# A list scheduler's cost numbers set to the durations of the profile, in a kernel of attention, experts and a dense network

## The chip, the cores and the metric

One core of one Trainium2 chip runs the kernel. The metric is the device time of one execution in microseconds (us); lower is better. Engines are named as in the profile: PE is TensorE (PEld its weight loads), ACT ScalarE, DVE VectorE, POOL GpSimd, SP SyncE, and a `q` behind a name is the engine's instruction queue.

## The reference

Three parts follow each other. `x` has 8 batches of 8 heads with 512 rows of 64 columns, `state` 32 rows for each head; the 8 x 544 rows that come out of the attention are the 4352 tokens of the rest.

```python
# attention, both ways, scale = 1 / sqrt(64)
a = softmax(scale * x @ state.T);   xread = a @ state
a2 = softmax(scale * state @ x.T);  sread = a2 @ x
x = concat([xread, sread], rows)                   # 4352 tokens of 512
# one expert of 8 for each token
logits = normalise(x) @ normalise(expert_emb).T / tau
e = argmax(logits);  gate = softmax(logits)[e]
x = gate * (relu(x @ w1[e]) @ w2[e])               # 512 -> 1024 -> 512
# dense network, for every token
h = x @ w_in                                       # 512 -> 2048
out = (h * clip(h + 3, 0, 6) / 6) @ w_out          # 2048 -> 512
```

All is float32, but `w_in` and `w_out`, which are float64.

## The kernel before

Big products are made of float32r parts: each operand is split in a high and a low part, and a product is three matmuls, high by high, low by high and high by low. So every operand costs a copy or cast that gives the high part (`wh`, `hx`, `yh`, `gh`, the first of `xt`) and a subtraction that gives the low part (`wl`, `yw`, `gl`, the second of `xt`).

**Stages.** The attention goes batch by batch, up to some 140 us. The routing then sorts the tokens by expert into slots of 128. The leading slots (`QUAD`, four slots, and `FIFTH`) are those of the expert with most tokens. The main units (`RUN`, one or two slots of one expert) follow: the products of `w1` (`L1w` line 1409, `L1` line 1450 for single slots), the relu and its split (`hx`, lines 1428 and 1432), the products of `w2` (`L2`, line 1512), the result times its gate (`yt`) and its store to `ysd` in sorted order (line 1540 on SP for the leading slots, line 1543 on POOL for the others). Beside them goes the dense network on blocks of 256 sorted tokens: load `yl` (line 1579), transpose (1585), split (`yh` 1594, `yw` 1597), `F1` (`u_ps`, line 1618), the activation (`r` 1622, `u_ps` 1625, `gh` 1629, `gl` 1632), `F2` (`o`, line 1653), and the result's scatter. What is left of the dense network when the units are done follows alone.

**Weights.** An expert's weights come as loads of `raw` (`load_w`, lines 1225 to 1252; the DMA on SP, line 1231 for `w1`, line 1234 for `w2`), through a ring of two buffers. Each load gives two pieces: `wh` (line 1245, by ACT or DVE) and `wl` (line 1248, by DVE or POOL), in a ring of three. The dense weights are converted once in 32 pieces (`convert`, lines 301 to 316): exponent and mantissa of the float64 are taken apart (lines 271 and 272 on DVE, 276 and 277 on ACT), multiplied (281 and 282 on DVE), summed (286, DVE or POOL) and split (293 ACT, 296 DVE or POOL). Eight of them come beside the attention, the others later.

**Tokens of a slot** (`X`, lines 1257 to 1384) are gathered by POOL (`xg` line 1270, in quarters `xq` line 1276) and turned into columns: by PE from a copy `xp` (line 1297) in the leading slots, by DVE's transposes of 32 x 32 (line 1314) in the others, whose cast `xt` (line 1325) goes to ACT or DVE and whose low part (line 1329) to DVE.

**What sets the order.** The kernel's instructions are written by a list scheduler (`Sched`, lines 39 to 151) that runs when the program is built. Every operation is given to it as `op(function, cost, priority, dependencies, buffers taken, buffers given, ...)`. The cost names the engine and a time in us; where it names two engines, the scheduler chooses. Each step takes the operation with the least key, where `b` is the time at which its operands, its buffers and its engine are ready by the scheduler's own clocks:

```python
key = (b + (c if len(o.cost) > 1 else 0.0) + self.wp * o.prio, o.prio)
```

It then sets `clk[e] = b + cost`, and the operation's end that much and `sem` later. For a DMA on SP's or ACT's queue the cost has a second meaning (line 142):

```python
self.hw = b + 0.45 * (1 + o.cost[e] // 0.12)
```

This is the time until which no other such DMA is issued: 0.45 us at a cost of 0.06, 1.8 us at 0.45. The priorities come from a nominal order (`at_`, `OFF`, `w_at`, `f1_at`) with numbers of its own.

## Time and profile before

| | |
|---|---|
| Runs | 1454.6 us median of 3 (1453.09 to 1455.71) |
| Span of the profiled execution | 1453.4 us, 1.2 us under the median |
| PE busy | 1354.7 us, 93% of the span |
| DVE busy | 917.8 us, 63% |
| ACT busy | 645.3 us, 44% |
| POOL busy | 543.1 us, 37% |

Only the span of the profiled execution is known, so it stands beside the median. The shares are means over stages that differ: the window table cuts the span into stages, with the busy time and, in brackets, the number of instructions of each engine. A line of a wait table names who waited, for whom, how long in total, how many times and the longest. A timeline's row has start, length, engine, line and operation, with idle time before it and its releaser in square brackets. A group of instructions by form has its busy time and the mean length of one in ns; a line's own table has least, median and greatest.

### The profile page before, as it was taken

How to read it: one execution, taken by the hardware profiler on the slowest of the kernel's cores; microseconds unless marked ns; L12 is line 12 of the kernel's file. 1: busy time of each engine (PE TensorE's matmuls, PEld its weight loads, DVE VectorE, ACT ScalarE, POOL GpSimd, SP SyncE). 2: the span in 40 equal slices, each digit the busy share in tenths (PEclk: the TensorE clock that was granted, in tenths of full speed). 3: DMA queues.
4: the chain of work that ended last, by engine and by line, in shares of the span. 5: the costliest groups of instructions: out<-in, count | busy, mean ns of one | idle time of the engine just before them, and what ended most of it. 6: DMA issues, size and time to landing. Idle time of an engine off the chain costs nothing. (4 is left out here: it accounts for less than half of the span.)

```text
span 1453.4 us, 25243 instructions
## 1 busy us (share of the span) xinstructions
PE 1354.7 (93%) x8976; PEld 1199.0 (82%) x8976; DVE 917.8 (63%) x2008; ACT 645.3 (44%) x1347; POOL 543.1 (37%) x558
## 2 busy tenths in 40 slices
PE   7896697877799999999999999999999999999997
PEld 6675686766688898989989898999998999899996
DVE  6988888899976555645454544665666675433332
ACT  4785435555643343434444343555544444333332
POOL 5554448566555232524142322244344322200000
PEclk8996689899899999999999999999999999999999
DMA  6643435555564333423243333555455544201000
GB/s 162 175 160 116 148 96 161 156 188 159 157 182 149 94 115 89 136 82 124 90 125 98 108 104 100 154 150 177 152 148 153 174 139 140 74 23 30 15 16 15
DMA packets 151765, 175.64 MB, mean 121 GB/s; under 512 B 43784, under 2 KB 116488, under 8 KB 150608
## 3 DMA queue, kind: packets, MB, share of 16 engines
q1 hardware_dynamic: 128544, 121.19, 28.2%
q0 software_dynamic: 12336, 35.99, 8.2%
q10 hardware_dynamic: 10752, 16.78, 3.6%
q8 instruction: 73, 1.20, 0.4%
q14 instruction: 60, 0.49, 0.1%
HBM read 146.09 MB, written 27.82 MB: 120 GB/s over the span
## 5 line engine op out<-in xcount | busy, mean ns | idle before, releaser
L1618 PE MATMUL u_ps<-yh,wih 128*128 128x256 f32 x1088 | 306.9, 282 | 6.0 <-DVE gl L1632 4.3
L1618 PE MATMUL u_ps<-yh,wil 128*128 128x256 f32 x1088 | 306.8, 282 | 3.1 <-DVE wil L296 3.1
L1618 PE MATMUL u_ps<-yw,wih 128*128 128x256 f32 x1088 | 307.0, 282 | 0.0
L1248 POOL TENSOR_TENSOR wl<-raw,wh 128x512 fp32r<-128x512 f32 x129 | 176.6, 1373 | 274.4 <-ACT wh L1245 127.3
L1625 DVE SCALAR_TENSOR_TENSOR u_ps<-r,u_ps 128x256 f32<-128x256 f32 x272 | 116.2, 427 | 255.0 <-ACT r L1622 240.5
L1622 ACT ACTIVATE r<-u_ps,three 128x256 f32<-128x256 f32 x272 | 129.1, 475 | 305.4 <-PE u_ps L1618 277.2
L1618 PEld LDWEIGHTS u_ps<-yh,wih 128*128 128x128 f32 x1088 | 207.3, 191 | 17.2 <-DVE gl L1632 4.3
L1653 PE MATMUL o<-woh,gh 128*128 128x512 f32 x544 | 217.0, 399 | 2.0 <-DVE yo L1667 1.2
L1653 PE MATMUL o<-wol,gh 128*128 128x512 f32 x544 | 216.4, 398 | 0.0
L1653 PE MATMUL o<-woh,gl 128*128 128x512 f32 x544 | 214.9, 395 | 0.0
L1618 PEld LDWEIGHTS u_ps<-yw,wih 128*128 128x128 f32 x1088 | 206.6, 190 | 8.5
L1618 PEld LDWEIGHTS u_ps<-yh,wil 128*128 128x128 f32 x1088 | 207.5, 191 | 3.3 <-DVE wil L296 3.3
L1512 PE MATMUL y_ps<-wh,hx 128*128 128x512 f32 x512 | 186.3, 403 | 1.3 <-DVE wh L1245 1.3
L1629 ACT CAST gh<-u_ps 128x256 fp32r<-128x256 f32 x272 | 101.2, 372 | 187.9 <-PE o L1653 140.4
L1248 DVE TENSOR_TENSOR wl<-raw,wh 128x512 fp32r<-128x512 f32 x223 | 160.5, 727 | 33.4 <-ACT wh L1245 29.6
L1632 DVE TENSOR_TENSOR gl<-u_ps,gh 128x256 fp32r<-128x256 f32 x272 | 114.4, 421 | 98.0 <-ACT gh L1629 94.3
L1276 POOL DMA_INDIRECT xq<-xd,qidx x128 | 136.1, 1063 | 54.0 <-issue 31.9
L1245 ACT CAST wh<-raw 128x512 fp32r<-128x512 f32 x197 | 120.9, 619 | 73.3 <-PE y_ps L1512 39.8
L1409 PE MATMUL h_ps<-xt,wh 128*128 128x256 f32 x704 | 140.9, 288 | 3.8 <-ACT wh L1245 3.8
L1672 POOL DMA_INDIRECT out_dram<-yo,ix x34 | 35.9, 1057 | 273.3 <-ACT gh L1629 160.0
L1653 PEld LDWEIGHTS o<-woh,gl 128*128 128x128 f32 x544 | 102.6, 189 | 25.2
L1409 PEld LDWEIGHTS h_ps<-xt,wh 128*128 128x128 f32 x704 | 117.6, 197 | 5.7 <-ACT wh L1245 4.2
(312 smaller groups left out, 2474.2 us busy)
## 6 DMA issues: line engine op xcount, KB each, us to landing
raw<-in_moe_w_dram SPq DMA_DIRECT2D x176, 512.0 KB
yl<-ysd SPq DMA_DIRECT2D x136, 64.0 KB
xd<-xr SPq DMA_DIRECT2D x8, 1056.0 KB
ysd<-yt POOLq DMA_DIRECT2D x32, 256.5 KB
xb<-in_x_dram SPq DMA_DIRECT2D x48, 128.0 KB
yw<-in_moe_w_out_dram ACTq DMA_DIRECT2D x9, 512.0 KB
cv_raw<-in_moe_w_in_dram ACTq DMA_DIRECT2D x8, 512.0 KB
yh<-in_moe_w_in_dram ACTq DMA_DIRECT2D x8, 512.0 KB
```

What stands on the lines that cost most here:

```text
L1245: copy[e](pc["hi"], box["t"][:, j, :])
L1248: eng[e].tensor_tensor(pc["lo"], box["t"][:, j, :], f32(pc["hi"]), op=ALU.subtract)
L1276: POOL.indirect_dma_start(q[:, j * QW:(j + 1) * QW], None, xd_q, index(qidx[:, j, s:s + 1]))
L1409: PE.matmul(out(f), pc[w][:, (2 * c + f) * 128:(2 * c + f + 1) * 128], u.xt[a][:, 2 * j + c, 256 * hf:256 * hf + 256], start=new and c == ...
L1512: PE.matmul(u.y[i], u.ht[t][:, a, lo + 128 * i:lo + 128 * i + 128], pc[w], start=c == 0 and k == 0, stop=c == KF - 1 and k == 2)
L1618: PE.matmul(p, w, y[:, k, :], start=k == 0 and j == 0, stop=k == KD - 1 and j == 2)
L1622: ACT.activation(q["r"], q["p"], AF.Relu, bias=pool["three"][:, 0:1])
L1625: DVE.scalar_tensor_tensor(q["p"], q["r"], 6.0, q["p"], op0=ALU.min, op1=ALU.mult)
L1629: ACT.copy(q["h"], q["p"])
L1632: DVE.tensor_tensor(q["l"], q["p"], f32(q["h"]), op=ALU.subtract)
L1653: PE.matmul(o["o"][a], g[:, a * 128:(a + 1) * 128], w, start=m == 0 and j == 0, stop=m == KFF - 1 and j == 2)
L1672: POOL.indirect_dma_start(out, bass.IndirectOffsetOnAxis(ap=o["ix"][:, a:a + 1], axis=0), box["t"], None)
```

## The change

Comments and docstrings are dropped, and the costs that are given to `op` are set to other numbers, for nearly every operation on ACT, DVE, POOL and SP and for the matmul groups of the units and of the dense network. Priorities, dependencies, buffers, rings, `wp`, `sem` and the scheduler stay. No instruction is added or taken away; what changes is the order in each queue and which engine does an operation that two can do. The core of the diff, with the operations that the prediction speaks of:

```diff
 def convert(n, prio, pool, ma, gate=None, start=0.0):
...
-        a = last_conv[0] = op(lambda: c.load(pool), {"A": 0.06}, prio - 8, [gate], [hr], dma=1.46, after=last_conv[0])
+        a = last_conv[0] = op(lambda: c.load(pool), {"A": 0.36}, prio - 8, [gate], [hr], dma=1.46, after=last_conv[0])
...
-        b = op(lambda: c.cs(ma), {"D": 0.67}, prio, [a], [hc])
-        d = op(c.ct, {"A": 1.13}, prio, [b])
-        e = op(c.cd, {"D": 1.2}, prio, [d])
+        b = op(lambda: c.cs(ma), {"D": 1.2}, prio, [a], [hc])
+        d = op(c.ct, {"A": 2.13}, prio, [b])
+        e = op(c.cd, {"D": 2.05}, prio, [d])
...
 def load_w(s, w, i, prio):
...
-        ld = last_raw[0] = op(load, {"S": 0.06}, prio[0] - 4, deps, [hr], dma=1.46, after=last_raw[0])
+        ld = last_raw[0] = op(load, {"S": 0.45}, prio[0] - 4, deps, [hr], dma=1.46, after=last_raw[0])
...
-            a = op(hi, {"A": 0.52, "D": 0.335}, prio[j], [ld], [pc["hold"]], [hr])
-            pc["op"] = op(lo, {"D": 0.6, "P": 1.225}, prio[j], [a], (), [hr])
+            a = op(hi, {"A": 0.62, "D": 0.42}, prio[j], [ld], [pc["hold"]], [hr])
+            pc["op"] = op(lo, {"D": 0.68, "P": 1.3}, prio[j], [a], (), [hr])
...
-            a = op(perm, {"A": 0.56, "D": 0.5}, prio, [og], [u.hx, hp] if i == 0 else [hp], [hg])
+            a = op(perm, {"A": 0.81, "D": 0.56}, prio, [og], [u.hx, hp] if i == 0 else [hp], [hg])
...
-            c = op(bh, {"A": 0.53, "D": 0.4}, prio, [b])
+            c = op(bh, {"A": 0.82, "D": 0.56}, prio, [b])
...
-        a = u.l1 = op(mm, {"T": 1.28}, prio, [*xd_, pc["op"]], u.h[q] if new else (),
+        a = u.l1 = op(mm, {"T": 1.4}, prio, [*xd_, pc["op"]], u.h[q] if new else (),
...
-        o["out"] = op(yd, {"S": 0.06} if u.lead else {"P": 1.04}, prio, ...
+        o["out"] = op(yd, {"S": 0.36} if u.lead else {"P": 1.1}, prio, ...
...
-            ld = last_y[0] = op(load, {"S": 0.3}, prio - 5.3354, deps, [hr] if a else [hr, o["ix"]], dma=0.8, after=last_y[0])
-            b = o["tr"] = op(tr, {"D": 0.602}, prio - 1.8572, [ld], [o["yT"]] if a == 0 else (), after=o.get("tr"))
-            c = op(hi, {"A": 0.478, "D": 0.335}, prio - 1.8572, [b])
-            o["ready"].append(op(lo, {"D": 0.602}, prio - 1.8572, [c], (), [hr]))
+            ld = last_y[0] = op(load, {"S": 1.9}, prio - 5.3354, deps, [hr] if a else [hr, o["ix"]], dma=0.8, after=last_y[0])
+            b = o["tr"] = op(tr, {"D": 0.71}, prio - 1.8572, [ld], [o["yT"]] if a == 0 else (), after=o.get("tr"))
+            c = op(hi, {"A": 0.62, "D": 0.42}, prio - 1.8572, [b])
+            o["ready"].append(op(lo, {"D": 0.69}, prio - 1.8572, [c], (), [hr]))
...
-        a = last_f[1] = op(mm, {"T": 1.306}, prio, [*o["ready"], dense.get(("i", m)), *deps], [hu],
+        a = last_f[1] = op(mm, {"T": 1.41}, prio, [*o["ready"], dense.get(("i", m)), *deps], [hu],
...
-        b = op(ra, {"A": 0.358}, prio, [a], [hr])
-        c = op(rb, {"D": 0.335}, prio, [b], (), [hr])
-        d = op(gh, {"A": 0.264}, prio, [c], [hg])
-        g_t[i, m] = op(gl, {"D": 0.335}, prio, [d], (), [hu]), hg, q
+        b = op(ra, {"A": 0.475}, prio, [a], [hr])
+        c = op(rb, {"D": 0.43}, prio, [b], (), [hr])
+        d = op(gh, {"A": 0.37}, prio, [c], [hg])
+        g_t[i, m] = op(gl, {"D": 0.43}, prio, [d], (), [hu]), hg, q
```

The others move alike: in the attention the copies from PSUM by about 0.1 us (`ca`, `cd`), `e2` from 0.664 to 0.89, `sd` from 3.06 to 3.6, `xr` from 0.491 (ACT) and 0.615 (DVE) to 0.6 and 0.69; in the units `hx` from 0.478 (ACT) and 0.602 (DVE) to 0.6 and 0.68, `L1` and `L2` from 0.645 to 0.7 for each slot; `F2` from 1.29 to 1.41.

**Where instructions move.** SP's queue at the end of the leading slots, before: `ysd<-yt` are the stores of the leading slots, `raw` the loads of the first main unit, `ix` and `yl` those of the first dense block.

```order
L1540 DMA ysd<-yt 128x513 x3
L1231 ISA
L1231 DMA raw<-in_moe_w_dram 128x4x256
L1540 DMA ysd<-yt 128x513 x2
L1231 ISA
L1231 DMA raw<-in_moe_w_dram 128x4x256
L1575 DMA ix<-ysd 128x2x1
L1579 DMA yl<-ysd 32x4x128 x8
L1234 ISA
L1234 DMA raw<-in_moe_w_dram 128x2x512
```

The same place after the change:

```order
L1540 DMA ysd<-yt 128x513 x5
L1231 ISA
L1231 DMA raw<-in_moe_w_dram 128x4x256
L1231 ISA
L1231 DMA raw<-in_moe_w_dram 128x4x256
L1575 DMA ix<-ysd 128x2x1
L1579 DMA yl<-ysd 32x4x128 x4
L1234 ISA
L1234 DMA raw<-in_moe_w_dram 128x2x512
L1579 DMA yl<-ysd 32x4x128 x4
```

The load of `raw` that had two stores behind it now has none, and the loads `yl` of the block, eight in a row before, are in two groups of four with a load of `raw` between them.

DVE's queue in the ramp, before, from the 15th `gl` (line 1632) of the dense network to the 16th:

```order
L1632 TENSOR_TENSOR gl<-u_ps,gh 128x256
L1248 TENSOR_TENSOR wl<-raw,wh 128x512
L281 SCALAR_TENSOR_TENSOR yh<-yh 128x512
L282 SCALAR_TENSOR_TENSOR cv_m<-yh,cv_m 128x512
L1625 SCALAR_TENSOR_TENSOR u_ps<-r,u_ps 128x256
L286 TENSOR_TENSOR cv_m<-cv_m,yh 128x512
L1248 TENSOR_TENSOR wl<-raw,wh 128x512
L1585 STREAM_TRANSPOSE yl<-yl 128x512
L1245 CAST wh<-raw 128x512
L296 TENSOR_TENSOR wol_3069<-cv_m,woh_3068 128x512
L1632 TENSOR_TENSOR gl<-u_ps,gh 128x256
```

And after the change, from the 15th to the 16th:

```order
L1632 TENSOR_TENSOR gl<-u_ps,gh 128x256
L296 TENSOR_TENSOR wol_3076<-cv_m,woh_3075 128x512
L1625 SCALAR_TENSOR_TENSOR u_ps<-r,u_ps 128x256
L1585 STREAM_TRANSPOSE yl<-yl 128x512 x2
L1632 TENSOR_TENSOR gl<-u_ps,gh 128x256
```

Two `wl` and a `wh` are gone from this place, and the conversion steps of lines 281, 282 and 286 stand further ahead; both transposes `yl` of a block stand in it instead of one.

POOL's queue in the ramp, before, up to the 40th quarter gather `xq` (eight for a pair of slots):

```order
L1248 TENSOR_TENSOR wl<-raw,wh 128x512 x4
L1270 DMA xg<-xd,gidx_79 128x528
L286 TENSOR_TENSOR cv_m<-cv_m,yw 128x512
L1248 TENSOR_TENSOR wl<-raw,wh 128x512
L296 TENSOR_TENSOR wol_3069<-cv_m,woh_3068 128x512
L1248 TENSOR_TENSOR wl<-raw,wh 128x512
L1270 DMA xg<-xd,gidx_79 128x528
L1276 DMA xq<-xd,qidx 128x132 x4
L1248 TENSOR_TENSOR wl<-raw,wh 128x512
L1276 DMA xq<-xd,qidx 128x132 x4
```

After the change, up to the same gather:

```order
L1248 TENSOR_TENSOR wl<-raw,wh 128x512
L1346 TENSOR_TENSOR nr<-nr,half 128x1
L1248 TENSOR_TENSOR wl<-raw,wh 128x512 x2
L286 TENSOR_TENSOR cv_m<-cv_m,yw 128x512
L1248 TENSOR_TENSOR wl<-raw,wh 128x512 x2
L286 TENSOR_TENSOR cv_m<-cv_m,yw 128x512
L1248 TENSOR_TENSOR wl<-raw,wh 128x512 x2
L1270 DMA xg<-xd,gidx_79 128x528 x2
L286 TENSOR_TENSOR cv_m<-cv_m,yw 128x512
L1248 TENSOR_TENSOR wl<-raw,wh 128x512 x3
L1276 DMA xq<-xd,qidx 128x132 x8
```

Seven `wl` stood in this piece, among the gathers, and ten stand in it now; the eight gathers `xq` come in one row behind them.

## Rows read from the trace of the kernel before

**Rows 1.** Window table: us, busy PE, PEld, DVE, ACT, POOL, PEclk, DMA share, GB/s

```profile
172.00:260.00 88.00, 77.81 (x437) 65.72 (x435) 69.69 (x157) 39.45 (x75) 52.61 (x45) 0.88 0.44 127
260.00:417.00 157.00, 123.09 (x653) 104.89 (x654) 150.41 (x245) 88.03 (x162) 99.07 (x77) 0.89 0.53 162
417.00:600.00 183.00, 180.28 (x1163) 162.64 (x1162) 104.14 (x247) 70.98 (x161) 63.84 (x64) 0.99 0.43 129
```

**Rows 2.** Waits of PE, 260 to 417 us: us in total, times, longest

```profile
PE y_ps L1512 <- POOL wl L1248: 6.8, 3, 4.1
PE y_ps L1512 <- DVE wl L1248: 5.7, 3, 2.7
PE h_ps L1409 <- DVE wl L1248: 5.3, 2, 3.4
PE h_ps L1409 <- POOL wl L1248: 5.1, 5, 1.6
```

**Rows 3.** Waits of DVE, 172 to 417 us

```profile
DVE hx L1432 <- ACT hx L1428: 6.9, 3, 3.3
DVE wh L1245 <- DMA raw<-in_moe_w_dram: 4.6, 3, 2.9
```

**Rows 4.** Line 1248 in the ramp: duration ns min/median/max, first and last start

```profile
L1248 POOL TENSOR_TENSOR wl<-raw,wh x27: 1264/1345/2103, 260.7 to 409.2; 128x512 fp32r<-128x512 f32 x27
...
L1248 DVE TENSOR_TENSOR wl<-raw,wh x16: 671/682/4239, 281.6 to 416.5; 128x512 fp32r<-128x512 f32 x16
```

**Rows 5.** Timelines of POOL and DVE: start, us, engine, line, operation

```profile
290.71 2.53 POOL L1248 TENSOR_TENSOR wl<-raw,wh 128x512 fp32r<-128x512 f32 x2
293.20 1.29 POOL L286 TENSOR_TENSOR cv_m<-cv_m,yw 128x512 f32<-128x512 f32 x1
...
290.81 4.24 DVE L1248 TENSOR_TENSOR wl<-raw,wh 128x512 fp32r<-128x512 f32 x1
```

**Rows 6.** Same stretch by form (busy us, mean ns), then lines 282 and 1329 with medians

```profile
L1248 DVE TENSOR_TENSOR wl<-raw,wh 128x512 fp32r<-128x512 f32 x16 | 15.5, 971 | 0.0
...
L282 DVE SCALAR_TENSOR_TENSOR cv_m<-yh,cv_m 128x512 f32<-128x512 uint16 x9 | 12.3, 1365 | 0.0
...
L1329 DVE TENSOR_TENSOR xt<-xq,xt 128x256 fp32r<-128x256 f32 x12 | 8.9, 783 | 0.0
...
L282 DVE SCALAR_TENSOR_TENSOR cv_m<-yh,cv_m x9: 719/732/3496, 276.8 to 403.2; 128x512 f32<-128x512 uint16 x9
...
L1329 DVE TENSOR_TENSOR xt<-xq,xt x12: 401/470/1515, 277.4 to 400.8; 128x256 fp32r<-128x256 f32 x12
```

**Rows 7.** Copies: whole run by form (busy us, mean ns); line 1325 with medians

```profile
L643 DVE TENSOR_TENSOR al<-a_ps,ah 128x1024 fp32r<-128x1024 f32 x7 | 8.5, 1217 | 1.6 <-ACT ah L637 1.6
...
L1297 DVE COPY xp<-xg 128x256 f32<-128x256 f32 x6 | 3.8, 693 | 0.0
...
L660 DVE COPY xr<-xr_ps 128x528 f32<-128x528 f32 x4 | 2.8, 699 | 0.7 <-PE xr_ps L657 0.7
...
L1325 DVE CAST xt<-xq x8: 278/306/3085, 398.1 to 552.4; 128x256 fp32r<-128x256 f32 x8
```

**Rows 8.** Timelines around the eleventh load: SP, then DVE, then PE

```profile
242.84 1.34 SPq L1540 DMA_DIRECT2D ysd<-yt  x3
244.44 0.40 SPq L1231 DMA_DIRECT2D raw<-in_moe_w_dram  x1
245.07 2.34 SPq L1540 DMA_DIRECT2D ysd<-yt  x2
...
253.32 5.22 SPq L1579 DMA_DIRECT2D yl<-ysd  x8
...
250.92 0.43 DVE L1245 CAST wh<-raw 128x512 fp32r<-128x512 f32 x1 [2.90 <-DMA raw<-in_moe_w_dram]
...
252.01 0.58 PE L1409 MATMUL h_ps<-xt,wl 128*128 128x256 f32 x1 [3.32 <-DVE wl L1248]
```

**Rows 9.** Waits of PE, 417 to 1254 us

```profile
PE y_ps L1512 <- DVE wh L1245: 1.3, 1, 1.3
```

More of the change, by code (lines that the diff above doesn't have):

```diff
@@ L780, in ca @@
         def ca(n):
-            return 0.052 + 0.000832 * n
+            return 0.16 + 0.00083 * n
         def cd(n):
-            return 0.064 + 0.00104 * n
+            return 0.15 + 0.00104 * n
         chunks = PARTS[1] if last else PARTS[0]
@@ L806, in batch @@
         for v in range(2):
-            e2.append(do("e2", o_e2, {"A": 0.664}, [mx[v]], [be2] if v == 0 else (), [hsc], args=(v,), late=v,
+            e2.append(do("e2", o_e2, {"A": 0.89}, [mx[v]], [be2] if v == 0 else (), [hsc], args=(v,), late=v,
                          after=e2[-1] if e2 else None))
-        r2 = do("r2", o_r2, {"D": 0.28}, e2)
-        sd = do("sd", o_sd, {"P": 3.06}, g_ready[b], [bsd])
+        r2 = do("r2", o_r2, {"D": 0.44}, e2)
+        sd = do("sd", o_sd, {"P": 3.6}, g_ready[b], [bsd])
         for (r0, r1), scs in zip(chunks, scs_):
@@ L840, in batch @@
                 lga_[b].append(do("lg", o_lg, {"D": 0.3}, [a], (), [hp], args=(r,), late=r))
-            w.append(do(f"x{r}c", o_xrc, {"A": 0.491, "D": 0.615}, [a], (), [hp], args=(r,), late=r))
+            w.append(do(f"x{r}c", o_xrc, {"A": 0.6, "D": 0.69}, [a], (), [hp], args=(r,), late=r))
         j = col(b)
@@ L1371, in X @@
             a = last_q[0] = op(parts, {"P": 4.16}, prio - 4, ready, [hq], dma=0.75, after=last_q[0])
-            b = u.tr = op(blocks, {"D": 0.66}, prio, [a], [u.hx] if i == 0 else (), after=u.tr)
-            c = op(bh, {"A": 0.53, "D": 0.4}, prio, [b])
-            u.x.append(op(bl, {"D": 0.67}, prio, [c], (), [hq]))
-        o1 = op(g1, {"D": 0.28}, late, [og], [hgate], [hg])
-        o2 = op(g2, {"A": 0.613}, late, [a if lead else og, o1], (), [hg])
-        o3 = op(g3, {"P": 0.464}, late, [o2])
-        o4 = op(g4, {"D": 0.34}, late, [o3, o1])
-        o5 = op(g5, {"A": 0.286}, late, [o4])
-        o["gate"] = op(g6, {"D": 0.27}, late, [o5], (), [hgate])
+            b = u.tr = op(blocks, {"D": 0.81}, prio, [a], [u.hx] if i == 0 else (), after=u.tr)
+            c = op(bh, {"A": 0.82, "D": 0.56}, prio, [b])
+            u.x.append(op(bl, {"D": 0.83}, prio, [c], (), [hq]))
+        o1 = op(g1, {"D": 0.32}, late, [og], [hgate], [hg])
+        o2 = op(g2, {"A": 0.82}, late, [a if lead else og, o1], (), [hg])
+        o3 = op(g3, {"P": 0.58}, late, [o2])
+        o4 = op(g4, {"D": 0.52}, late, [o3, o1])
+        o5 = op(g5, {"A": 0.49}, late, [o4])
+        o["gate"] = op(g6, {"D": 0.31}, late, [o5], (), [hgate])
         if lead:
@@ L1456, in relu @@
             ACT.activation(u.hs[v], u.hp[v], AF.Relu)
-        a = u.l1 = op(mm, {"T": 0.645}, prio, [*u.x, pc["op"]], [u.h[v]] if k % 4 == 0 else (), [pc["hold"]], after=u.l1)
+        a = u.l1 = op(mm, {"T": 0.7}, prio, [*u.x, pc["op"]], [u.h[v]] if k % 4 == 0 else (), [pc["hold"]], after=u.l1)
         if k % 4 == 3:
-            u.r[v] = op(relu, {"A": 0.478}, prio, [a], (), [u.h[v]])
+            u.r[v] = op(relu, {"A": 0.6}, prio, [a], (), [u.h[v]])
             if u.lead:
@@ L1481, in HT @@
         a = u.l1 = op(tr, {"T": 0.434}, prio, [u.r[v]], [hm, hh], [u.hx] if v else (), after=u.l1)
-        b = op(hi, {"A": 0.478}, prio, [a])
-        u.r["t", v] = op(lo, {"D": 0.602}, prio, [b], (), [hm])
+        b = op(hi, {"A": 0.59}, prio, [a])
+        u.r["t", v] = op(lo, {"D": 0.69}, prio, [b], (), [hm])
     last_out = [None]
@@ L1543, in yd @@
                 POOL.dma_start(ysd[bass.ds(cv, 128), :], o["yt"])
-        b = op(ya, {"A": 0.571}, prio, [a, o["gate"]], [hy], [yh])
-        c = op(yb, {"D": 0.07}, prio, [b])
-        o["out"] = op(yd, {"S": 0.06} if u.lead else {"P": 1.04}, prio, [b, c, None if u.lead else cs_op] + ([] if u.lead else [slots[k]["out"] for k in range(NL)]),
+        b = op(ya, {"A": 0.69}, prio, [a, o["gate"]], [hy], [yh])
+        c = op(yb, {"D": 0.15}, prio, [b])
+        o["out"] = op(yd, {"S": 0.36} if u.lead else {"P": 1.1}, prio, [b, c, None if u.lead else cs_op] + ([] if u.lead else [slots[k]["out"] for k in range(NL)]),
                       (), [hy], dma=0.73, after=None if u.lead else last_out[0])
@@ L1654, in mm @@
                               start=m == 0 and j == 0, stop=m == KFF - 1 and j == 2)
-        f = last_f[2] = op(mm, {"T": 1.29}, prio, [ready, dense.get(("o", m)), *deps],
+        f = last_f[2] = op(mm, {"T": 1.41}, prio, [ready, dense.get(("o", m)), *deps],
                            o["acc"] if m == 0 else (), [hg], after=last_f[2])
```

24 lines of the change are left out of this document (12 added, 12 removed).

## The prediction

> **What bounds the kernel now.** I read the window table by stage first. From 417 to 1254 us TensorE has next to no gaps (180.28 of 183.00 us busy in the first piece of it), and what follows is TensorE alone, so a new order can gain almost nothing there. Between 260 and 417 us TensorE is busy 123.09 of 157.00 us while VectorE is busy 150.41: this is the ramp, where the float64 weights are still being converted beside the expert pieces, and VectorE is the engine that paces it. From 172 to 260 us (the leading slots) VectorE is busy 69.69 of 88.00 us and TensorE 77.81 [rows 1]. The waits of TensorE in the ramp come second: four of them end on a `wl`, the low part of an expert weight, 11.9 us with GpSimd's and 11.0 us with VectorE's [rows 2]. Third the waits of VectorE over both stages: they are small and end on ScalarE or on a load of `raw` [rows 3]. So the question is what the new order does to VectorE between 172 and 417 us, and to the few queues that feed it.
>
> **What the change does to the order.** No instruction is added or removed; larger cost numbers give other moments, so other orders and, where two engines can do an operation, other engines. TensorE's own order stays nearly as it was. Counted in the order up to the 17th `gl`, which ends the ramp: VectorE does 8 `wl` fewer (20 for 28), 3 `wh` fewer, 4 casts `xt` more, 2 copies `xp` more, and in the attention one `xr` and one `xT` copy more. GpSimd and ScalarE take or give the same ones.
>
> **The sum, term by term**, against the span of 1453.4 us, which lies 1.2 us under the median of the runs; I add the sum to the median 1454.6.
>
> (1) *The eight `wl` that move to GpSimd.* One takes 0.68 us on VectorE at the median and 1.345 on GpSimd [rows 4]. The most it can give is 8 x 0.68 = 5.4 us. But the two engines get in each other's way. At 290.81 us a `wl` on VectorE, which began 0.10 us behind two on GpSimd, took 4.24 us and ended half a microsecond after the GpSimd work that followed those two (293.20 + 1.29 = 294.49) [rows 5]. It is no single case: in the ramp VectorE's `wl` has a mean of 0.971 us against a median of 0.682, `cv_m` of line 282 1.365 against 0.732, `xt` of line 1329 0.783 against 0.470. That is 16 x 0.289 + 9 x 0.633 + 12 x 0.313 = 14.1 us of stretching, and GpSimd ran 27 `wl` meanwhile: 0.52 us lost for each, if I put it all down to them [rows 4, 6]. So a moved `wl` gives 0.68 - 0.52 = 0.16 us, and eight give **-1.3**. Ends: -5.4 with no stretching at all, and +5.3 if each blocks VectorE for all of its 1.345 us (8 x (1.345 - 0.68)). I take the middle because it is what this ramp shows on average.
>
> The Trainium skill (SBUF — State Buffer, section Who interferes with whom) says that a VectorE instruction with two inputs in SBUF contends with a GpSimd instruction that reads SBUF, and that the one that issued first keeps the shared port for its whole length while the other waits. The row at 290.81 us agrees. By this rule taken to its end, the eight moved operations would cost VectorE 5.3 us instead of giving 1.3; that is the case of the port below.
>
> (2) *`wh` and `xt` in the ramp.* Three `wh` fewer at 0.43 us [rows 8] are -1.3, four `xt` casts more at 0.306 us +1.2 [rows 7]: together **-0.1**.
>
> (3) *More copies on VectorE before the ramp.* Two `xp` at 0.693, an `xr` at 0.699 and an `xT`, which VectorE has not done here; the nearest row is `al` with the same 128x1024 at 1.217. Together 3.3 us [rows 7]. VectorE is not full there (79% of its time in the leading slots) and ScalarE is relieved of as many, so between 0 and +3.3; I take a third, **+1.1**.
>
> (4) *The load behind the stores.* On SP's queue the eleventh load of `raw`, the third piece of the first main unit, now stands behind all five stores of the leading slots instead of three. Before, it was issued at 244.44 us, the last two stores ended at 247.41 [rows 8], so it leaves 3.0 us later. It has no cover: VectorE already waited 2.90 us for it and TensorE 3.32 us for the `wl` made of it [rows 8]. So **+3.0**. Ends: 0, if another gap of the leading slots shrinks by as much, and +6.5, the time from that issue to the cast at 250.92, if the load's transfer is also held up by the stores. I take the row's own shift. Further on that queue the second half of the first block's `yl` stands behind the next load: that load is issued 2.6 us sooner (half of the 5.22 us), the half block some 0.4 us later (one issue). I cost it at nothing, as TensorE has twelve more products of the unit ahead of the first `u`; without that cover it is +0.4.
>
> (5) *After 417 us.* Over the program VectorE does 31 `wl` fewer. TensorE's longest wait after 417 us is 1.3 us on a `wh` from VectorE [rows 9]; I let it go: **-1.3**. Ends: 0 and -2.7, all of TensorE's idle time from 417 to 600 us (183.00 - 180.28) [rows 1].
>
> The attention's products, the routing and all of the dense network keep their places on TensorE; I cost their moves at nothing, since what goes before them on VectorE has the same total apart from (3). The sum: -1.3 - 0.1 + 1.1 + 3.0 - 1.3 = **+1.4 us, so 1456.0 us**. About 0.2% (2.9 us) is what a measurement of this kernel can tell from no change; +1.4 is inside.
>
> **The rivals.**
>
> *The order gets better as a whole.* The old numbers had VectorE and ScalarE too fast (a conversion step reckoned at 0.67 us and now at 1.2), so the scheduler kept putting work in front that was not yet ready. If the truer numbers halve VectorE's idle time from 172 to 417 us, (88.00 - 69.69) + (157.00 - 150.41) = 24.9 us, 12.4 us are won, less the 3.0 of the late load: -9.4, so 1445.2. For it: 11.5 us of VectorE's waits there are on `hx` from ScalarE and on `raw`, which an order can change [rows 3]. Against it: the counts above show that nearly the same work stands ahead of each step of the ramp, and VectorE is already 96% busy in it.
>
> *GpSimd becomes the late one* (slower). A weight piece goes `raw`, `wh`, `wl`, product. On GpSimd the last step takes 1.345 - 0.68 = 0.67 us longer, and the gathers stand in the same queue. TensorE already waited 11.9 us, in eight waits, for `wl` from GpSimd, out of 27 [rows 2, 4]. If all of the eight moved ones end a wait, 8 x 0.67 = 5.4 us come on top of +1.4: 1461.4. It decides from the point where most moved pieces, not 8 in 27, are the last thing a product waits for. At the old rate it would be 8/27 of it, 1.6 us.
>
> *The port takes back more than the move gives.* Term (1) is +5.3 and not -1.3, so +8.0 in all: 1462.6. For it: the 4.24 us row; against it: the median `wl` in the ramp is undisturbed.
>
> *The change does nothing to the end.* All moves lie in slack, 1454.6. Against it: the load of (4) had no slack.
>
> **How the numbers follow.** Forecast 0.40, the better order 0.29, late GpSimd 0.17, the port 0.08, nothing 0.06. The forecast's own range is 1446 to 1463: -5.4 - 0.1 + 0 + 0 - 2.7 = -8.2, and -1.3 - 0.1 + 3.3 + 6.5 + 0 = +8.4. Of its 0.40 I put 0.06 on faster by over 0.2%, 0.22 within, 0.12 slower, as its upper end reaches as far as its lower but its centre is above zero. So faster 0.06 + 0.29 = 0.35, within 0.22 + 0.06 = 0.28, slower 0.12 + 0.17 + 0.08 = 0.37. The range goes from the better order without the late load (1454.6 - 12.4 = 1442) to the port's case with all of term (3) (1462.6 + 2.2 = 1465).
>
> **What would show it.** In the profile after: between 260 and 417 us, or where the 17th `gl` now ends, VectorE has some 20 `wl` and GpSimd some 8 more; if the mean `wl` on VectorE rises well above 0.97 us the port's case holds. The eleventh `raw` load should leave some 3 us later against the third store, and TensorE's wait behind it should be near 6 us and not 3.3. TensorE's waits for GpSimd's `wl` should stay near 12 us; 17 or more speaks for the second rival. VectorE's idle time from 172 us to the end of the ramp should stay near 25 us; if it is near 12, the first rival was right. The prediction is wrong if the time differs by more than these terms while the ramp's end stays within 2 us of 417: then the difference comes from the attention or from the dense part, which I cost at nothing.

## The result: 1.2% slower, and the profile after

The changed kernel takes 1473.27 us (median of 4 runs, 1469.43 to 1474.7) against 1454.51 us before: +18.8 us, ratio 1.0122, 95% interval 1.0105 to 1.0139. My forecast was 1456.0, no change, in a range of 1442 to 1465. The profiled execution has a span of 1472.8 us, 19.4 us over the one before.

(One correction to the section on the kernel: the scheduler's class is lines 39 to 128, and the formula for the gap of two DMA issues is line 118.)

The first view is again the window table, cut at the same times as [rows 1]: us, busy time of PE, PEld, DVE, ACT and POOL, the granted clock, the DMA share, GB/s.

```profile
172.00:260.00 88.00, 73.99 (x412) 60.92 (x410) 69.26 (x153) 36.86 (x71) 56.81 (x48) 0.90 0.39 113
260.00:417.00 157.00, 116.01 (x625) 97.62 (x625) 135.53 (x220) 83.32 (x149) 96.98 (x72) 0.87 0.52 159
417.00:600.00 183.00, 179.04 (x1110) 159.86 (x1111) 99.07 (x232) 74.19 (x170) 80.02 (x77) 0.98 0.42 125
600.00:1254.00 654.00, 652.28 (x4203) 588.58 (x4202) 388.35 (x873) 273.60 (x618) 253.80 (x232) 1.00 0.43 129
```

Read it against [rows 1]: TensorE is busy 3.8 us less in the leading slots (73.99 for 77.81), 7.1 less in the ramp (116.01 for 123.09) and 1.2 less up to 600 us. From there to 1254 us it has next to no gaps, as before. So some 12 of the 19 us are lost between 172 and 600 us, and nothing that comes later gives them back. The starts of the same matmuls in the two traces say it too: the one of line 1618 that stood at 526.6 us is 13.7 us late, the last products of line 1512 are 15.3 us late, and what follows the branch, which is shown below, 19.4. The second thing to see is VectorE in the ramp: 135.53 us where it had 150.41. I had called it the engine that paces the ramp. It now has 21.5 us of idle time there, and the ramp is slower.

Where TensorE waits in the same 157 us, the view of [rows 2]:

```profile
PE h_ps L1409 <- POOL wl L1248: 10.5, 5, 4.0
PE y_ps L1512 <- POOL wl L1248: 9.7, 8, 2.6
PE h_ps L1409 <- DVE wh L1245: 5.1, 1, 5.1
PE o L1653 <- ACT woh L293: 4.8, 1, 4.8
PE y_ps L1512 <- ACT wh L1245: 4.4, 3, 1.6
PE y_ps L1512 <- DVE wl L1248: 2.4, 1, 2.4
```

For GpSimd's `wl` it is 20.2 us in 13 waits and was 11.9 in 8; for VectorE's `wl` 2.4 and was 11.0. The sum of the two is nearly the same (22.6 for 22.9): the pieces are not later in sum, they are late on another engine. What is new stands beside them: `wh` of the late load and `woh` of a dense piece. ScalarE's `wh` is not new (4.4 us; 3.8 before, on `h_ps`), and what TensorE waited for `gl` of the dense network, 4.3 us before, is gone.

What the two engines did with `wl` in that stretch, as in [rows 4], and its form on VectorE, as in [rows 6]:

```profile
L1248 POOL TENSOR_TENSOR wl<-raw,wh x32: 1254/1350/2164, 266.1 to 415.8; 128x512 fp32r<-128x512 f32 x32
...
L1248 DVE TENSOR_TENSOR wl<-raw,wh x7: 674/681/693, 263.3 to 349.3; 128x512 fp32r<-128x512 f32 x7
```

```profile
L1248 DVE TENSOR_TENSOR wl<-raw,wh 128x512 fp32r<-128x512 f32 x7 | 4.7, 682 | 0.0
L1329 DVE TENSOR_TENSOR xt<-xq,xt 128x256 fp32r<-128x256 f32 x12 | 4.3, 413 | 0.0
```

Five `wl` more on GpSimd and nine fewer on VectorE at the same clock time. The seven that VectorE kept were not stretched at all (mean 0.682, maximum 0.693 us; before 0.971 and 4.239), and `xt` of line 1329 fell from a mean of 0.783 to 0.413 us. But the stretching did not go away, it went to other operations: to the conversion above all, as in the low part of a dense weight, before and after:

```profile
L296 DVE TENSOR_TENSOR wil<-cv_m,wih 128x512 fp32r<-128x512 f32 x7 | 4.8, 681 | 0.2 <-ACT wih L293 0.2
...
L296 DVE TENSOR_TENSOR wil<-cv_m,wih 128x512 fp32r<-128x512 f32 x8 | 10.8, 1353 | 0.1
```

Over all of VectorE's operations in the ramp, the time beyond the shortest fifth of each form sums to 38.9 us before and 35.4 after (an estimate from the rows of the two traces). If that is all the port's, it took about as much as before, with nine `wl` fewer on VectorE.

SP's queue at the end of the leading slots, to be read beside [rows 8]; after it, TensorE's row for the product of the first main unit that waits for the piece of the late load (a wait of 5.09 us, 3.32 before):

```profile
246.45 9.34 SPq L1540 DMA_DIRECT2D ysd<-yt  x5
256.04 1.07 SPq L1231 DMA_DIRECT2D raw<-in_moe_w_dram  x2
257.22 0.43 SPq L1575 DMA_DIRECT2D ix<-ysd  x1
257.77 3.56 SPq L1579 DMA_DIRECT2D yl<-ysd  x4
264.63 0.40 SPq L1234 DMA_DIRECT2D raw<-in_moe_w_dram  x1
265.29 2.12 SPq L1579 DMA_DIRECT2D yl<-ysd  x4
```

```profile
263.42 0.55 PE L1409 MATMUL h_ps<-xt,wh 128*128 128x256 f32 x1 [5.09 <-DVE wh L1245]
```

The five stores took 9.34 us, since the last one stood waiting for its tile: the tile's index column was written on VectorE at 255.25 us only, behind a `wl` of 1.70 us:

```profile
253.62 1.70 DVE L1248 TENSOR_TENSOR wl<-raw,wh 128x512 fp32r<-128x512 f32 x1
255.25 0.14 DVE L1536 COPY yt<-oidx 128x1 int32<-128x1 int32 x1
```

The load behind them left at 256.04 us, 11.6 us later than before, and not 3.0. The stores are not all of it. The load needs a buffer of `raw`, and the last reader of that buffer is a `wl` that ran on VectorE before and on GpSimd now, and ends 8.3 us later (243.48 and 251.77 us); before, then after:

```profile
242.81 0.67 DVE L1248 TENSOR_TENSOR wl<-raw,wh 128x512 fp32r<-128x512 f32 x1
...
250.51 1.26 POOL L1248 TENSOR_TENSOR wl<-raw,wh 128x512 fp32r<-128x512 f32 x1
```

So the load was held twice, by the `wl` up to 251.8 us and by the stores up to 256.0. The first `u` of the dense network started at 276.3 us (266.1 before).

These rows show how a place in an in-order queue costs time. GpSimd's and TensorE's timelines:

```profile
363.51 2.03 POOL L286 TENSOR_TENSOR cv_m<-cv_m,yh 128x512 f32<-128x512 f32 x1 [6.25 <-DVE cv_m L282]
365.51 3.40 POOL L1248 TENSOR_TENSOR wl<-raw,wh 128x512 fp32r<-128x512 f32 x2
...
389.62 2.07 POOL L286 TENSOR_TENSOR cv_m<-cv_m,yw 128x512 f32<-128x512 f32 x1 [4.43 <-DVE cv_m L282]
```

```profile
367.27 0.79 PE L1512 MATMUL y_ps<-wl,hx 128*128 128x512 f32 x1 [2.56 <-POOL wl L1248]
...
392.39 0.80 PE L1653 MATMUL o<-woh,gh 128*128 128x512 f32 x1 [4.82 <-ACT woh L293]
```

Up to 363.5 us GpSimd did nothing for 6.25 us, because the next operation in its queue was a step of a dense weight's conversion that VectorE had not fed yet. Two `wl` stood behind that step, and TensorE waited 2.56 us for the first. At 392 us it is the converted piece itself that is late, by 4.82 us.

The last 4 us are lost where the program branches past the slots that may be empty. From TensorE's timeline and, for the twelve matmuls, the chain that ended last:

```profile
1272.14 0.55 PE L1618 MATMUL u_ps<-yh,wih 128*128 128x256 f32 x1 [3.61 <-PEq L1827]
1272.49 0.41 PE L1618 MATMUL u_ps<-yw,wih 128*128 128x256 f32 x1
```

```profile
1272.14 2.90 PE u_ps L1618 x12
...
1276.53 1.43 PE u_ps L1618 x12
```

Window table of the changed kernel behind the branch, with the granted clock in the column behind POOL:

```profile
1272.10:1275.00 2.90, 2.86 (x13) 2.89 (x14) 0.00 (x0) 0.00 (x0) 0.00 (x0) 0.50 0.07 6
1276.00:1279.00 3.00, 3.00 (x21) 2.70 (x20) 0.93 (x3) 0.85 (x2) 0.00 (x0) 1.00 0.45 101
```

TensorE's sequencer took 3.61 us there and 0.88 before. Behind the longer pause the granted clock was 0.50, the lower of the two levels (1.2 GHz), and the first twelve matmuls took 2.90 us where twelve take 1.43 later. In the kernel before the clock stayed at 1.00 and those twelve took 1.52 us (1254.10 to 1255.62). That is 2.7 + 1.4 = 4.1 us. Why the branch took longer is not shown.

### The profile page after: what moved, and what is told of

The parts are those of the page before. It is cut to its first block, busy times and chain, and to the rows that moved or that the text cites. A ratio compares the mean times of both kernels' runs of the same rounds, so it can differ in the third digit from the quotient of the medians.

```text
span 1472.8 us, 25297 instructions
## 1 busy us (share of the span) xinstructions
PE 1357.5 (92%) x8976; PEld 1196.9 (81%) x8976; DVE 918.2 (62%) x2000; ACT 632.8 (43%) x1324; POOL 593.7 (40%) x589
## 5 line engine op out<-in xcount | busy, mean ns | idle before, releaser
L1248 POOL TENSOR_TENSOR wl<-raw,wh 128x512 fp32r<-128x512 f32 x160 | 223.6, 1403 | 318.2 <-ACT wh L1245 138.2
L1248 DVE TENSOR_TENSOR wl<-raw,wh 128x512 fp32r<-128x512 f32 x192 | 139.4, 738 | 30.4 <-ACT wh L1245 25.2
L1245 ACT CAST wh<-raw 128x512 fp32r<-128x512 f32 x188 | 114.4, 619 | 59.4 <-PE y_ps L1512 31.1
L1512 PEld LDWEIGHTS y_ps<-wh,hx 128*128 128x128 f32 x512 | 99.6, 195 | 28.4 <-ACT wh L1245 6.1
```

Source lines behind the costliest of these rows:

```text
L1245: copy[e](pc["hi"], box["t"][:, j, :])
L1248: eng[e].tensor_tensor(pc["lo"], box["t"][:, j, :], f32(pc["hi"]), op=ALU.subtract)
L1512: PE.matmul(u.y[i], u.ht[t][:, a, lo + 128 * i:lo + 128 * i + 128], pc[w], start=c == 0 and k == 0, stop=c == KF - 1 and k == 2)
```

## The experiments

Three theories stood first. **Late GpSimd**: the moved `wl` are what TensorE waits for. **The load behind the stores**: the queue on SP. **The order as a whole**: no single move. Every comparison below is with the kernel before, timed beside it on the same chip.

### Only the engines of `wl`, with every order kept (runs 1 and 2)

In the code, each `wl` is handed to the engine that the scheduler chose. In these two runs a table overrules the choice at the moment of writing the instruction, so all else stands exactly where it stood.

```diff
-                eng[e].tensor_tensor(pc["lo"], box["t"][:, j, :], f32(pc["hi"]), op=ALU.subtract)
+                eng[FIX.get((s, w, 2 * i + j), e)].tensor_tensor(pc["lo"], box["t"][:, j, :], f32(pc["hi"]), op=ALU.subtract)
```

The table, left out here, names 19 pieces of the first four main units: 14 move one way and 5 the other. Run 1, the changed kernel with the engines of before:

> The order of the changed kernel on every queue, but the wl of the first four main units (slots 5 to 12) are run by the engine that ran them before the change: 14 go from GpSimd back to VectorE, 5 the other way. Theory 'late GpSimd': TensorE's waits for GpSimd's wl between 260 and 530 us, 24.7 us in the changed kernel against 11.8 before, are most of the 13 us that the ramp loses, so they fall to near 12 us and the time falls by 8 to 12 us, to about 1463. Theory 'load behind the stores': nearly nothing, 1471 to 1475. Theory 'the order as a whole': the pieces are late on either engine because VectorE's queue is in another order, a gain of 0 to 4 us.

1470.94 us, ratio 1.0121 (1.0098 to 1.0144): 2.3 us below the changed kernel's median, and by the ratios, which stand to the kernel before as timed beside each, no difference at all (1.0122). The first theory, which wanted 8 to 12 us, fails here as the whole cause. Nor did the waits for GpSimd's `wl` fall to near 12 us, as it had said: they are 19.1 us between 172 and 530 us, and 26.6 in the changed kernel. TensorE's waits there:

```profile
PE y_ps L1512 <- POOL wl L1248: 14.3, 6, 6.7
PE y_ps L1512 <- DVE wl L1248: 6.6, 3, 3.7
PE h_ps L1409 <- DVE wh L1245: 5.3, 2, 3.2
PE h_ps L1409 <- POOL wl L1248: 4.8, 4, 2.9
```

Run 2, the kernel before with the changed kernel's engines:

> The counterpart: the order of the kernel before on every queue, with the engines for wl of the changed kernel in the first four main units (14 from VectorE to GpSimd, 5 the other way). Theory 'late GpSimd': slower by 8 to 12 us, about 1464, with TensorE's waits for GpSimd's wl near 25 us. Theory 'load behind the stores' and theory 'the order as a whole': within 4 us of 1454.5.

1466.45 us, ratio 1.0094 (1.0072 to 1.0116): +11.4 us, as the first theory had it. The same view:

```profile
PE y_ps L1512 <- POOL wl L1248: 16.0, 6, 5.1
PE h_ps L1409 <- POOL wl L1248: 13.5, 7, 6.0
```

29.5 us of waits for GpSimd's `wl`, against 11.9 before. So what the engine of a piece is worth depends on the order around it: in the order of before the moved pieces cost 11.4 us; in the changed order, which was made with those engines in mind, putting them back repairs some 2.3 by the medians, and the waits move to other pieces.

### Only the place of one load (runs 3 and 4)

Run 3 writes the last two stores of the leading slots behind the eleventh load of `raw`, run 4 (in the kernel before) writes that load behind all five stores. Nothing else moves.

```diff
-                SP.dma_start(ysd[s * 128:(s + 1) * 128, :], o["yt"])
+                late.append((s, o["yt"])) if s > 2 else SP.dma_start(ysd[s * 128:(s + 1) * 128, :], o["yt"])
...
-                SP.dma_start(t.rearrange("p a (c f) -> p (a c) f", c=2), src)
+                SP.dma_start(t.rearrange("p a (c f) -> p (a c) f", c=2), src); [SP.dma_start(ysd[q * 128:(q + 1) * 128, :], y) for q, y in (late if (s, i) == (5, 2) else ())]
```

> The changed kernel, only that on SP's queue the last two stores of the leading slots stand behind the eleventh load of raw instead of in front of it, as in the kernel before; every other queue keeps its order. Theory 'load behind the stores': the load leaves some 6 to 10 us sooner than at 256.0 us, the first u of the dense network starts near 268 and not 276 us, and the time falls by 5 to 10 us. Theory 'late GpSimd': the first u starts sooner too, but the ramp then waits for wl and under 3 us are left of it at the end.

1470.77 us, ratio 1.0128 (1.0104 to 1.0152): by the medians 2.5 us of the 18.8 come back, by the ratios nothing that can be told from none. But the run did not do to the load what it was meant to: the load left only 3.0 us sooner than in the changed kernel, and the first `u` started at 277.9 us, not near 268.

```profile
253.01 0.40 SPq L1231 DMA_DIRECT2D raw<-in_moe_w_dram  x1
```

With the stores out of its way it waited 4.4 us for the `wl` on GpSimd that holds its buffer. In run 1 it is the other way round: that `wl` is back on VectorE and ends at 248.1 us, but the stores hold the load until 254.79. Each of the two runs takes away one of two holders of the same load, and no run takes away both. So what the two theories are worth together is open.

> The counterpart: the kernel before, only that the eleventh load of raw stands behind all five stores. My prediction priced this at 3.0 us (0 to 6.5). Theory 'load behind the stores': slower by 3 to 10 us, with the first u of the dense network later by as much. Theory 'late GpSimd': slower by under 3 us.

1458.46 us, ratio 1.0027 (1.0013 to 1.0041): 3.45 us by the medians. The load left at 248.62 us, 4.2 us later than before:

```profile
243.87 4.55 SPq L1540 DMA_DIRECT2D ysd<-yt  x5
248.62 0.40 SPq L1540 DMA_DIRECT2D raw<-in_moe_w_dram  x1
```

This is the one term of my sum that came out as priced: 3.0 forecast, 3.45 measured by itself (1.9 to 6.0 by the interval).

### Undoing groups of costs in the changed kernel (runs 5 to 8)

The theories now were about the cost numbers: their second meaning in the gap of DMA issues (run 5), durations that are no rates (run 6), the conversion (run 7), the attention (run 8). Run 6 needs a row. On VectorE a `wl` is 0.68 us long, yet two of them take 1.29 us (VectorE's timeline of the kernel before, below), so the second starts 0.61 us behind the first. The old cost 0.6 is the distance of two starts, the new 0.68 the length.

```profile
251.26 1.29 DVE L1248 TENSOR_TENSOR wl<-raw,wh 128x512 fp32r<-128x512 f32 x2
```

```diff
-                    self.hw = b + 0.45 * (1 + o.cost[e] // 0.12)
+                    self.hw = b + 0.45 * (1 + o.cost[e] // 0.65)
```

> All new costs, but the scheduler's formula for the gap between two DMA issues has 0.65 in place of 0.12, so a load of raw (cost 0.45) and a store (0.36) hold the modelled issue for 0.45 us again and not for 1.8, and the four loads yl (1.9) for 1.35 and not 7.2. The trace shows gaps of about 0.65 us from one issue to the next. Theory 'second meaning': the raised SP costs made the scheduler think that loads are issued late, and so mis-order what waits for them; most of the loss goes, 1455 to 1462. Theory 'durations are not rates' (the costs of VectorE's operations are now 0.07 us longer than the distance of two starts, so the model has VectorE too slow): under 4 us, 1469 or more. Theory 'any new order is worse than the one kept': between 1460 and 1475.

1475.94 us, ratio 1.0162 (1.0131 to 1.0194). Not better; of the theories only that of run 6 had left room for it (1469 or more). The load stands in front of three of the stores here and the branch takes 0.7 us, but TensorE's waits for GpSimd's `wl` are 19.5 us between 172 and 530 us.

Run 6 sets back the costs of 29 lines of the diff, such as `{"A": 0.62, "D": 0.42}` to `{"A": 0.52, "D": 0.335}` for `wh`:

> The changed kernel with the old costs for the casts, subtractions, copies and gate steps of units, tokens and dense blocks (the groups of wh, wl, xt, xp, hx, yt, yh, yw, r, gh, gl, yo); the new ones stay for the attention, the conversion of the dense weights, the DMAs on SP and the matmuls. Theory 'durations are not rates': a wl on VectorE is 0.68 us long but two of them start 0.61 apart, so with 0.6 the model is right again, VectorE gets its wl back (287 over the program, 275 before, 244 with the change) and most of the loss goes, 1455 to 1462. Theory 'second meaning' and theory 'conversion': under 4 us of the 16 to 19 come back.

1471.07 us, ratio 1.0126 (1.0091 to 1.0162): the same as the changed kernel within the intervals. VectorE has its `wl` back over the program, but in the ramp it has six and GpSimd 34.

Run 7 sets back three lines:

```diff
-        b = op(lambda: c.cs(ma), {"D": 1.2}, prio, [a], [hc])
-        d = op(c.ct, {"A": 2.13}, prio, [b])
-        e = op(c.cd, {"D": 2.05}, prio, [d])
+        b = op(lambda: c.cs(ma), {"D": 0.67}, prio, [a], [hc])
+        d = op(c.ct, {"A": 1.13}, prio, [b])
+        e = op(c.cd, {"D": 1.2}, prio, [d])
```

> The changed kernel with the old costs of the three middle steps of a weight's conversion (0.67, 1.13 and 1.2 us in place of 1.2, 2.13 and 2.05; the trace has about 1.2, 2.2 and 2.1). Theory 'conversion': the model now keeps VectorE and ScalarE longer with conversion in the ramp and so gives wl to GpSimd; with the old numbers VectorE has 28 wl at the 17th gl as in the kernel before, and the ramp's loss (10 to 13 us) goes, 1458 to 1463. The other theories: 1468 to 1475.

1488.08 us, ratio 1.0245 (1.0214 to 1.0276): 15 us worse than with the new costs of the conversion, and outside what any theory had.

Run 8 sets back the nine lines of the attention (`ca`, `cd`, `e2`, `r2`, `sd`, `nm`, `a2c`, `sx`, `xr`):

> The changed kernel with the old costs of the attention. In the changed kernel the first matmuls of the leading slots' second product stand some 3 us behind those before by 207 us, and TensorE waits 4.0 us for xp from VectorE where it waited 1.4. Theory 'attention': those 3 us come back, 1467 to 1471, and nothing more. The other theories: no change from the new attention costs, 1470 to 1475.

1496.54 us, ratio 1.0294 (1.0261 to 1.0326), the slowest of all, 23 us over the changed kernel, by costs of a stage that ends at 140 us; no theory had that either. All four theories fail as the cause. Undoing a part of the change does not lead back towards the kernel before; it gives another order, and each of them is worse than 1455.

### Small moves of one number (runs 9 to 12 and 18)

That asked for a measure of what any new order costs. Each of these changes one number by little; `sem` is the lag from one operation's end to the next one's start.

```diff
-    sc.wp, sc.sem = 0.0473, 0.6218
+    sc.wp, sc.sem = 0.0473, 0.6343
```

> The kernel before with one number of the scheduler moved by 2% (the lag from one operation's end to the next one's start, 0.6218 to 0.6343, in the units and the dense network). It makes the model neither truer nor less true in a way that matters. Theory 'any new order is worse than the one kept': the order of before stands at a good point and its neighbours do not, so this alone makes the kernel slower by 5 to 25 us. Theory 'the changed costs themselves are wrong' (by any of the mechanisms named so far): within 4 us of 1454.5.

1457.82 us, ratio 1.0017 (1.0003 to 1.0031): 2.5 us slower. That is less than the 5 to 25 us of the theory 'any new order'; it falls where the other theory had it.

> The kernel before with the scheduler's lag 2% lower (0.6218 to 0.6094), the neighbour on the other side of the ninth run (1457.8 with 2% more). Theory 'any new order is worse than the one kept': slower by 2 to 20 us here, too. If it is faster than 1455 by more than 3 us, the order of before is no chosen point and that theory falls.

1459.13 us, ratio 1.0029 (1.0017 to 1.0042), with 0.6094: 4.5 us slower, within the 2 to 20 us.

> The kernel before with only the cost of a wl on GpSimd raised by 2% (1.225 to 1.25; the trace has a median of 1.345, so it is truer). Theory 'any new order is worse than the one kept': slower by 5 to 25 us. Theory 'the changed costs themselves are wrong': within 4 us of 1454.5, or a little faster.

```diff
-            pc["op"] = op(lo, {"D": 0.6, "P": 1.225}, prio[j], [a], (), [hr])
+            pc["op"] = op(lo, {"D": 0.6, "P": 1.25}, prio[j], [a], (), [hr])
```

1466.11 us, ratio 1.0078 (1.0056 to 1.0099): a cost moved by 0.025 us, in the right direction, costs 10.8 us. Here TensorE waits no longer for GpSimd than before (11.7 us from 172 to 530 us), but on other things:

```profile
PE u_ps L1618 <- DVE gl L1632: 12.3, 4, 6.1
PE h_ps L1409 <- DVE wl L1248: 10.7, 5, 3.3
PE y_ps L1512 <- DVE wl L1248: 8.2, 2, 6.8
```

> The changed kernel with the same 2% on the lag (0.6218 to 0.6343). Theory 'any new order': it lands anywhere between some 1460 and 1490, on either side of 1473. Theory 'the changed costs themselves': within 4 us of 1473.

1483.14 us, ratio 1.0189 (1.0169 to 1.021): 10 us over the changed kernel.

> The changed kernel with the lag lowered by 0.07 us (0.6218 to 0.5518), by which the new costs of VectorE and ScalarE are longer than the distance of two starts: so that cost and lag together are again what they were. Theory 'the lag is now counted twice': faster than the changed kernel by 5 to 15 us. Theory 'any new order': between 1460 and 1490, on either side of 1473.

1490.04 us, ratio 1.0229 (1.02 to 1.0259): 17 us over it, against the theory that the lag was now counted twice. TensorE's longest sum of waits is one that the kernel before does not have:

```profile
PE o L1653 <- ACT woh L293: 15.4, 4, 4.6
PE h_ps L1409 <- POOL wl L1248: 9.4, 5, 2.7
PE h_ps L1409 <- DVE wh L1245: 7.0, 2, 5.8
```

### One group of the new costs alone (runs 13 to 17)

The change cut in five groups that together are all of it, each alone in the kernel before. The edits are those of the diff above, of these lines alone: the matmul groups; the DMAs on SP, the load of a dense piece and, in the same line of code as the stores on SP, GpSimd's stores (1.04 to 1.1); the casts, subtractions, copies and gate steps; the attention; the three middle steps of a conversion.

> The kernel before with the new costs of the matmul groups alone (L1w 1.28 to 1.4, L1 and L2 0.645 to 0.7, F1 1.306 to 1.41, F2 1.29 to 1.41; in the trace 12 F1 matmuls take 1.43 us and 6 of F2 1.41). Theory 'one group of costs carries the loss': one of the five groups run alone lies near 1473 and the rest within 4 us of 1455. Theory 'any new order': each group alone lies between 1456 and 1470, as the 2% moves did (1458 and 1466), and the groups do not add up to the whole.

> The kernel before with the new costs of the DMA issues alone (raw 0.06 to 0.45, the stores of the leading slots 0.06 to 0.36, yl 0.3 to 1.9, the load of a dense piece 0.06 to 0.36), by which the formula for the gap of two issues gives 1.8 us and more. All five stores stand ahead of the loads here, too, so it has at least the 3.4 us of the fourth run. Theory 'one group' with these as the cause: near 1473. Theory 'any new order': 1458 to 1470.

> The kernel before with the new costs of the casts, subtractions, copies and gate steps alone, the counterpart of the sixth run, with the last three steps of a conversion. Over the program VectorE has 223 wl, the fewest of all. Theory 'one group' with these as the cause (durations that are not rates): near 1473, with TensorE's waits for GpSimd's wl above 20 us between 260 and 530. Theory 'any new order': 1456 to 1470.

> The kernel before with the new costs of the attention alone, the counterpart of the eighth run (which was 23 us slower than the changed kernel). Theory 'the new attention costs are good': faster than 1455 by some us, or the same. Theory 'any new order': 1456 to 1470. The first matmul of the leading slots' second product stands at 207.5 us in the kernel before and 210.7 in the changed one; here it tells how much of it is the attention's.

> The kernel before with the new costs of the three middle steps of a conversion alone (1.2, 2.13 and 2.05 us), the fifth and last group. The four others gave +4 to +27 us by themselves. Theory 'one group of costs carries the loss' has no place left in which it holds; theory 'any new order': between 1456 and 1485.

| group alone | median, us | against before, timed beside it | ratio, 95% interval |
|---|---|---|---|
| matmuls | 1475.99 | +20.5 | 1.0139 (1.0108 to 1.0170) |
| DMA issues | 1482.60 | +27.1 | 1.0178 (1.0144 to 1.0213) |
| casts, subtractions, gates | 1481.88 | +26.4 | 1.0181 (1.0149 to 1.0212) |
| attention | 1459.28 | +3.8 | 1.0019 (1.0004 to 1.0033) |
| conversion | 1475.50 | +20.8 | 1.0134 (1.0115 to 1.0154) |
| all five, the change | 1473.27 | +18.8 | 1.0122 (1.0105 to 1.0139) |

The parts sum to +98.6 us and the whole is +18.8. No group carries the loss, and four of five are worse alone than all together. I had expected 1456 to 1470 for a scatter; three of the four groups of which I had said so lie above that, so the scatter is wider than I thought. What differs is again where TensorE waits. With the conversion's costs alone, 172 to 530 us:

```profile
PE u_ps L1618 <- DVE gl L1632: 16.7, 7, 9.0
PE y_g L1512 <- DVE wl L1248: 8.5, 1, 8.5
PE h_ps L1409 <- DVE wl L1248: 6.1, 4, 2.6
```

GpSimd's `wl` is hardly waited for here (7.4 us); the dense network's `gl` and a piece of the leading slots are.

The run with the attention's costs alone also answers what its expectation asked: the first matmul of the leading slots' second product stands at 211.2 us there, so these costs by themselves are enough for the 3.2 us between 207.5 and 210.7.

**What the eighteen show together.** All eighteen are slower than the kernel before, by 2.5 to 42.5 us, and the changed kernel stands tenth of the nineteen by its median's distance. The six that are the kernel before with little moved (a 2% move, one load, the engines of 19 pieces, the attention's costs) lie 2.5 to 11.4 us above it, the twelve others 16 to 42.5. In fourteen of the eighteen profiles TensorE is busy 717.7 to 719.5 of the 720 us from 530 to 1250 us, as in the kernel before (718.9) and the changed one (718.3), so most of their loss is made ahead of that (and, in some, at the branch). In four it is not: runs 5, 11, 12 and 18 have 716.5, 713.0, 713.7 and 714.7. In run 18 TensorE is 0.4 us ahead of the kernel before at the matmul that stood at 579 us, and 3.3 behind at the one of 687, so its loss owes nothing to the ramp. In the waits that I show the loss is on other pieces each time.

That fits an order of before that sits at a good point of the scheduler's numbers, off which nearly every step is worse. How it came to sit there no run shows, only that both neighbours in `sem` and every other one tried are worse. Nor do the runs part "moved" from "raised": every run that sets new costs in the kernel before raises them, nearly without exception, and none lowers them; only `sem` was moved both ways. No version beat both kernels. Whether `wp`, `sem` and the priorities could be set anew so that the new costs give a better order than the old ones is open: I tried two other values of `sem` with the new costs, and both were worse.

## Why the prediction was wrong

Its step that failed is the sentence that priced the rest of the order: "I cost their moves at nothing", with "nearly the same work stands ahead of each step of the ramp" as the reason given against the first rival. Equal counts do not make equal times: a queue runs in order, and what matters is which operation stands behind one that still waits, as the two `wl` behind the starved conversion step at 363 us. I priced five moves at +1.4 us and left all others at zero, and +18.8 was measured. Undoing the engines of `wl` or the place of the load gave back 2.3 and 2.5 us, and 4.1 are lost at the branch; the rest was not traced to single moves, and what the first two give together was not run. What the runs do show in place of "nothing" is that moves of this kind have a price: 2.5 to 11.4 us for one small number, place or set of engines, and 3.8 to 27.1 us for a group of the new costs.

Term by term:

- Term (1), the eight `wl`, -1.3 us: the size and the sign were wrong. It was reckoned as work taken off VectorE. In the order of before the engines alone cost +11.4 us (run 2, 19 pieces of four units, so somewhat more than the eight up to the 17th `gl`). The price that counts is the later `wl` for whoever waits for it (the product, and at 251.8 us the buffer of the next load), not VectorE's time: VectorE has 21.5 us of idle time in the changed ramp and that bought nothing. The reading under it, that VectorE paces the ramp because it is 96% busy, fell with it.
- The port in term (1) was read from three forms, 14.1 us of stretching. By all forms it was 38.9 us, and 35.4 with the change: on `wl` it fell away (0.682 us for 0.971), on the conversion it rose. So a price for each moved `wl` from the mean of `wl`, in the middle or at either end (-5.4, +5.3), was the wrong measure: an operation on VectorE pays when it begins while one on GpSimd runs (the counts are in the last section). The port's case, whose sign was a mean of `wl` well above 0.97, did not come.
- Term (2), -0.1, was not tried by itself. Term (3), +1.1, has the right sign: in the changed kernel TensorE waits 4.0 us for `xp` from VectorE before the first product where it waited 1.4 us. Its upper end, 3.3, was nearer than the third of it that I took: the leading slots' second product starts 3.2 us later, and run 16, the attention's costs alone, is 3.8 us slower.
- Term (4), the load behind the stores, +3.0: right in mechanism and size by itself (3.45 us, run 4). In the changed kernel the load left 11.6 us later. I had taken the old end of the last store, which now waits for its tile, and had not seen that a `wl` of term (1) holds the buffer of this load. The sum took the terms one by one, and these two meet; taking the stores away alone moved the load by 3.0 us and gave 2.5 us back by the medians.
- Term (5), -1.3 after 417 us: TensorE is busy 180.28 us from 417 to 600 us in [rows 1] and 179.04 in the view after; nothing was gained there, and 4.1 us were lost at the branch, on which the prediction has no term.

The second rival, late GpSimd, had the right sign, and what I had named for it stands in the profile: 20.2 us of waits in the ramp, above the 17 that I had named, and 13 of 32 pieces waited for, 8 of 27 before. Its price, 6.8 us over the median, was too small, and run 1 speaks against its being all of it. The first rival, a better order by truer numbers, had 0.29 from me and is the reverse of what the runs show: VectorE's idle time from 172 to 417 us went from 24.9 to 40.2 us ((88.00 - 69.26) + (157.00 - 135.53)), not to 12.

## What to carry to other kernels

Costs read from a trace do not by themselves give a list scheduler a better order: any change of a cost gives another order, and here a 2% change of one cost was worth 11 us, one of another number 2.5 to 4.5. So measure first what a neutral change of the scheduler's numbers does, and judge an edit that moves every queue against that spread, or set the other numbers anew with it. And undo two suspects together as well as one by one: here two of them held the same load, so undoing one alone could not show what it was worth. An engine that is busy 96% of a stretch is not thereby what sets its length; ask which operand ends the wait of the engine whose gaps are lost.

## What the runs showed of the hardware

- VectorE's operations overlap at their ends: a `wl` is 0.68 us long, two in a row take 1.29 us. A cost for a queue of them is 0.61 us and not the length of the row.
- The stretching of VectorE's two-input operations beside GpSimd depends on how the two line up. In the two ramps, of the 137 operations of lines 286, 296, 282, 1248, 1329 and 1597 on VectorE, 37 began while a subtraction or sum of 128x512 ran on GpSimd, and 36 of these took over 1.3 times their usual length; of the 100 others 3 did. All of the 36 but one, the row of 4.24 us, ended 0.54 to 0.56 us behind the end of that GpSimd operation (some 0.28 us in line 1329, whose tiles are half as wide), whatever was left of it. So each waited for the whole of it. The Trainium skill (SBUF — State Buffer, section Who interferes with whom) puts it on which of the two issued first, and these counts agree with that.
- In the changed kernel a pause of 3.61 us of TensorE was paid twice: the granted clock behind it was 0.50 for the next 2.9 us. Behind the pause of 0.88 us in the kernel before it was 1.00. The second payment is not fixed by the pause: behind 3.67 us in run 1 the clock fell some 0.7 us into the matmuls, behind 3.35 us in run 3 some 1.2.
